# Constants of a decode kernel loaded at the end of the first key row instead of by a load of their own

## The chip, the cores and the metric

The kernel runs on one core of a Trainium2 chip. The metric is device time in microseconds (us) per execution; "span" is the time from the first to the last event in a profile, a little over 1 us less. Engines are called as in the profile: PE (matrix multiply, with PEld for its weight loads), DVE, ACT (ScalarE), POOL, and SP (SyncE), which here only issues loads. Loads are carried out by DMA engines, 16 by the page's count; a load has landed when an engine that waits for it sees its completion.

## The reference, cut to what matters

Two layers of attention and MLP decode one token. Each of 32 heads reads the last W = 4096 keys and values of 192 numbers each, so almost all the work is reading caches and weights.

```python
x = A_x                                   # 1 x 1 x 640, bf16
for layer in range(2):                    # the same weights and caches twice
    x = x + attention(layernorm(x), k_cache[:, :, -4096:], v_cache[:, :, -4096:], wq, wo)
    x = x + mlp(layernorm(x), w_gate, w_up, w_down)
```

## The kernel before

Heads are worked on in 16 pairs. SBUF holds one array, `big`, with seven slots of UNIT = 14208 bf16 per partition (28416 bytes) and a shared region behind them. A slot holds a pair's wq and keys ("a"), or its values and wo ("b"). Two thirds of the bytes come in loads ("c") that fill two neighbouring slots at once: keys of pair p and values of pair p-1, in rows of 56832 bytes on each of 128 partitions. SP issues every load in one fixed order, each as soon as its slots are free.

One small load is different. The constants (identity, masks, selectors and x itself, 241 bf16 or 482 bytes per partition) go into a tile of their own, on ScalarE's queue:

```python
cst = sb("cst", [P, CE + CE % 2], BF16)                   # CE = 241
big = sb("big", [P, NSLOT * UNIT + ME], BF16, 256)
M0 = NSLOT * UNIT                                          # start of the shared region
...
pg.dma(q_dma(cst[:, 0:CE], cx), "x", wr=[res("cst")], q="adma")   # ScalarE's queue
while seq_pos[0] < 2:                                      # SP: keys of pair 0, then ("c", 0, 1)
    assert try_load(seq[seq_pos[0]])
    seq_pos[0] += 1
pg.op("pool", ... tensor_copy(slot(2, wo of pair 0), slot(5, wo of pair 0)))
...
# first users of the constants: they start pair 0
pg.op("dve", ... wsel from pm, rd=[res("cst")])
pg.op("dve", ... xT[0] and its sum from x_in, rd=[res("cst")], ...)
```

Pair 0 then goes: layernorm sums, projection of q (Q), scores (QK), maximum, exp, transposed exp (ET). Pair 1 repeats this, with the values of pair 0 in between (PV). Slots for the fourth load come free only when pair 1's softmax has passed and pair 0's output has been projected.

## Time and profile before

| | before |
|---|---|
| time, median of the first 3 executions | 513.91 us (513.4 to 514.08) |
| span | 512.3 us |
| busy: PE, DVE, ACT | 51%, 20%, 17% |
| read from memory | 218.2 MB at a mean of 426 GB/s |
| first use of the constants | 15.31 us |
| first key load landed, after its issue at 0.0 | 11.0 us |

These lines of the page show what bounds the kernel. The slices are 40 equal parts of the span; a 9 is 90% busy or more. The queue lines give packets, MB and the share of the DMA engines' time; q1 is SP's queue and q10 is ScalarE's.

```profile
span 512.3 us, 8586 instructions
...
DMA  9999999999999999999999999999999999999996
...
GB/s 422 435 423 426 423 426 436 426 426 448 444 430 435 432 430 430 430 426 453 409 413 418 409 441 431 434 435 426 435 448 444 439 426 426 431 436 417 427 429 283
...
q1 hardware_dynamic: 9506, 218.14, 99.2%
...
q10 hardware_dynamic: 144, 0.06, 0.0%
```

In slices of this size the DMA engines are busy 90% or more until the last one. Busy time by stretch says it for the long middle part (columns: stretch, length, busy us and instructions of PE, PEld, DVE, ACT, POOL, granted PE clock, DMA share, GB/s):

```profile
0.00:30.00 30.00, 7.30 (x80) 4.01 (x84) 4.50 (x22) 3.45 (x6) 2.04 (x6) 1.00 1.01 426
...
60.00:250.00 190.00, 88.28 (x1179) 43.86 (x1183) 31.29 (x111) 27.70 (x55) 1.07 (x12) 0.59 1.00 433
```

The timeline of the start (start us, length us, engine, line, operation, count, and in brackets the idle time before and what ended it). The last line is SP's issue of the fourth load.

```profile
0.78 0.38 ACTq L217 DMA_DIRECT2D cst<-in_cx_dram  x1
...
15.31 0.17 DVE L364 TENSOR_SCALAR sc<-cst 128x2 f32<-128x2 bf16 x1 [13.20 <-DMA cst<-in_cx_dram]
...
17.43 2.75 PE L432 MATMUL scores<-big,qs 128*32 128x512 bf16 x24 [0.35 <-DVE qs L420]
...
24.72 0.38 PE L464 MATMUL bank<-cst,e_sb 128*128 128x8 bf16 x8 [1.98 <-ACT e_sb L458]
...
27.91 0.56 PE L414 MATMUL bank<-sh,big 128*128 128x1 bf16 x15 [2.81 <-DMA big<-in_uc_dram]
...
33.82 1.47 PE L494 MATMUL o<-big,et_sb 128*2 128x384 bf16 x32
...
37.98 0.33 SPq L217 DMA_DIRECT2D big<-in_uc_dram  x1
```

The constants, issued at 0.78 us, release DVE at 15.31 us, though the keys of pair 0 were there at about 11. Pair 0's scores start at 17.43 and its ET ends at about 25.1. PE then waits 2.81 us for the second load, and pair 1 starts at 27.91.

The chain of waits (start, length, what), its first load and the next:

```profile
1.17 44.86 DMA big<-in_uc_dram
...
57.90 21.63 DMA big<-in_uc_dram
```

It starts with 45 us of loads. Pair 0 is not on it.

### The profile page before, as it was taken

How to read it: one execution, taken by the hardware profiler on the slowest of the kernel's cores; microseconds unless marked ns; L12 is line 12 of the kernel's file. 1: busy time of each engine (PE TensorE's matmuls, PEld its weight loads, DVE VectorE, ACT ScalarE, POOL GpSimd, SP SyncE). 2: the span in 40 equal slices, each digit the busy share in tenths (PEclk: the TensorE clock that was granted, in tenths of full speed). 3: DMA queues.
4: the chain of work that ended last, by engine and by line, in shares of the span. 5: the costliest groups of instructions: out<-in, count | busy, mean ns of one | idle time of the engine just before them, and what ended most of it. 6: DMA issues, size and time to landing. Idle time of an engine off the chain costs nothing.

```text
span 512.3 us, 8586 instructions
## 1 busy us (share of the span) xinstructions
PE 260.4 (51%) x3716; PEld 137.8 (27%) x3716; DVE 102.3 (20%) x386; ACT 85.2 (17%) x173; POOL 4.3 (1%) x31
## 2 busy tenths in 40 slices
PE   0452456333534464436576767775726343534655
PEld 0220222121212231223234434432312121212334
DVE  0221322112210221112121333231202112210312
ACT  1110111011101111011121023221201011101221
POOL 0010000000000000000000000000000000000000
PEclk9995655567755565666555568865665557755575
DMA  9999999999999999999999999999999999999996
GB/s 422 435 423 426 423 426 436 426 426 448 444 430 435 432 430 430 430 426 453 409 413 418 409 441 431 434 435 426 435 448 444 439 426 426 431 436 417 427 429 283
DMA packets 9670, 218.47 MB, mean 426 GB/s; under 512 B 1201, under 2 KB 1586, under 8 KB 4658
## 3 DMA queue, kind: packets, MB, share of 16 engines
q1 hardware_dynamic: 9506, 218.14, 99.2%
q8 instruction: 13, 0.21, 0.1%
q10 hardware_dynamic: 144, 0.06, 0.0%
q14 instruction: 7, 0.06, 0.0%
HBM read 218.20 MB, written 0.00 MB: 426 GB/s over the span
## 4 chain that ended last, share of the span: by engine, by line
DMA 63%; PE 24%; DVE 7%; ACT 3%; issue 2%; SPq 1%; DVEq 0%; POOL 0%; ACTq 0%; POOLq 0%
DMA big<-in_uc_dram 54%; PE scores L432 8%; PE o L494 7%; DMA big<-in_wd_dram 6%; DMA big<-in_wu_dram 4%; DVE sc L442 3%; PE bank L448 2%; PE bank L414 2%; ACT e_sb L458 2%; PE bank L529 1%; PE bank L464 1%; ACT diag L445 1%; SPq L217 1%; DVE sc L477 1%; DVE qs L420 1%
## 5 line engine op out<-in xcount | busy, mean ns | idle before, releaser
L432 PE MATMUL scores<-big,qs 128*32 128x512 bf16 x744 | 82.7, 613 | 10.3 <-DVE qs L420 9.5
L414 PE MATMUL bank<-sh,big 128*128 128x1 bf16 x465 | 17.2, 166 | 133.1 <-DMA big<-in_uc_dram 130.7
L494 PE MATMUL o<-big,et_sb 128*2 128x384 bf16 x1024 | 73.7, 453 | 7.2 <-DMA big<-in_uc_dram 4.1
L445 ACT ACTIVATE diag<-cst,sc 128x128 f32<-128x128 bf16 x32 | 12.8, 401 | 308.3 <-DVE sc L442 295.1
L442 DVE TENSOR_REDUCE sc<-scores 128x1 f32<-128x1024 f32 x31 | 37.9, 1224 | 78.3 <-PE scores L432 78.3
L414 PEld LDWEIGHTS bank<-sh,big 128*128 128x128 bf16 x465 | 14.8, 104 | 136.2 <-DMA big<-in_uc_dram 113.6
L448 PE MATMUL bank<-diag,sc 128*128 128x128 f32 x64 | 22.1, 441 | 46.6 <-ACT diag L445 46.6
L458 ACT ACTIVATE e_sb<-scores,sc 128x1024 bf16<-128x1024 f32 x31 | 37.4, 1206 | 41.6 <-DVE sc L453 39.3
L420 DVE TENSOR_TENSOR qs<-bank,cst 128x96 bf16<-128x96 f32 x30 | 7.7, 258 | 162.0 <-PE bank L414 162.0
L494 PEld LDWEIGHTS o<-big,et_sb 128*2 128x2 bf16 x1024 | 27.3, 104 | 41.2 <-issue 25.8
L432 PEld LDWEIGHTS scores<-big,qs 128*32 128x32 bf16 x744 | 24.1, 132 | 43.7 <-issue 31.2
L448 PEld LDWEIGHTS bank<-diag,sc 128*128 128x128 f32 x64 | 13.8, 269 | 72.7 <-ACT diag L445 70.5
L501 ACT CAST o_sb<-o 128x384 bf16<-128x384 f32 x64 | 29.4, 475 | 19.8 <-PE o L494 19.6
L529 PE MATMUL bank<-sh,big 128*128 128x1 bf16 x480 | 17.2, 165 | 15.4 <-DVE sh L518 15.4
L468 DVE CAST et_sb<-bank 128x64 bf16<-128x64 f32 x32 | 7.2, 225 | 68.1 <-PE bank L464 68.1
L529 PEld LDWEIGHTS bank<-sh,big 128*128 128x128 bf16 x480 | 14.6, 99 | 17.9 <-DVE sh L518 12.5
L449 DVE TENSOR_REDUCE sc<-bank 128x2 f32<-128x128 f32 x32 | 9.3, 292 | 42.8 <-PE bank L448 42.8
L464 PE MATMUL bank<-cst,e_sb 128*128 128x8 bf16 x256 | 11.7, 169 | 8.2 <-ACT e_sb L458 8.1
L464 PEld LDWEIGHTS bank<-cst,e_sb 128*128 128x128 bf16 x256 | 8.9, 101 | 24.0 <-issue 17.1
L475 PE MATMUL o<-sc 128*128 128x2 f32 x62 | 14.2, 298 | 0.6 <-ACT o_sb L501 0.6
L475 PEld LDWEIGHTS o<-sc 128*128 128x128 f32 x62 | 12.1, 244 | 2.2 <-ACT o_sb L501 1.3
L477 DVE RECIPROCAL sc<-o 64x1 f32<-64x1 f32 x62 | 10.2, 165 | 10.5 <-PE o L475 8.7
(81 smaller groups left out, 110.9 us busy)
## 6 DMA issues: line engine op xcount, KB each, us to landing
big<-in_uc_dram SPq DMA_DIRECT2D x20, 7104.0 KB, 22.7
big<-in_uc_dram SPq DMA_DIRECT2D x11, 3552.0 KB, 20.1
big<-in_uc_dram SPq DMA_DIRECT2D x2, 3072.0 KB, 17.9
big<-in_uc_dram SPq DMA_DIRECT2D x8, 480.0 KB, 6.3
big<-in_uc_dram SPq DMA_DIRECT2D x1, 2784.0 KB, 12.2
big<-in_uc_dram SPq DMA_DIRECT2D x1, 2304.0 KB, 10.3
big<-in_uc_dram SPq DMA_DIRECT2D x1, 2048.0 KB, 10.8
big<-in_wg_dram SPq DMA_DIRECT2D x2, 960.0 KB, 15.9
```

Of the source, the lines that this page charges most:

```text
L414: ins = t.matmul(qe[:, i:i + 1], lhsT=w[:, c * 2 * DH + c0:c * 2 * DH + c0 + P], rhs=xq[:, c:c + 1], start=(c == 0), stop=(c == DC - 1))
L432: ins = t.matmul(sc_x[1 + b][32 * j:32 * j + 32, :], lhsT=qs[:, y, k, :], rhs=slot(sa, WQE + k * W + (4 * b + j) * 512, 512), start=(k == ...
L442: pg.op("dve", lambda v: v.reduce_max(out=mx, in_=sc_x[0][:], axis=AX.X), wr=[res("mx")], ex=sc_x[3:5])
L445: pg.op("act", lambda a: a.mul(out=diag[:], in_=ident, mul=mx), rd=[res("cst"), res("mx")], wr=[res("diag")])
L448: pg.op("pe", lambda t: t.matmul(dmx[:, 0:P], lhsT=ones_f, rhs=diag[:], start=True, stop=True), rd=[res("diag"), res("ones")], ex=[rb[2]])
L458: pg.op("act", lambda a: a.activation(out=e_sb[:], in_=sc_x[0][:], func=ACT.Exp, bias=nbias, scale=srs_c, accum_out=rowsum), rd=[res("nbia ...
L464: ins = t.matmul(qe[:, 0:2 * NB].rearrange("p (r x) -> p r x", r=2)[:, :, 4 * b:4 * b + 4], lhsT=e_sb[:, b * P:(b + 1) * P], rhs=sel, star ...
L475: pg.op("pe", lambda t: t.matmul(sm, lhsT=ones_f, rhs=rs2[z], start=True, stop=True), rd=[res(f"rs2{z}"), res("ones")], wr=[res("rsum")], ...
L477: rb[bk].last["dve"] = pg.op("dve", lambda v, h=h: v.reciprocal(out=Rn[z][64 * h:64 * h + 64], in_=sm[64 * h:64 * h + 64, h:h + 1]), rd=[r ...
L494: ins = t.matmul(o8[h][32 * j:32 * j + 2, 0:2 * DH].rearrange("p (a d) -> p a d", a=2), lhsT=et_sb[:, z, h * NB + 2 * u:h * NB + 2 * u + 2 ...
L501: pg.op("act", lambda a, h=h: a.copy(out=o8_sb[:, :, h * DH:(h + 1) * DH], in_=o8[h][:, 0:2 * DH].rearrange("p (a d) -> p a d", a=2)), wr= ...
L529: ins = t.matmul(yT[:, j:j + 1], lhsT=wo[:, c * D + j * P:c * D + (j + 1) * P], rhs=oTb[z][:, c:c + 1], start=False, stop=(c == 2), skip_g ...
```

## The change

The intent: let the constants come with the first key load, so that the small load on the second queue goes away and pair 0 can start earlier. The array gets a gap of 256 bf16 behind the slot of the first keys, the host writes the constants behind the first key row in memory, and the first key load becomes 241 columns longer.

```diff
-    cst = sb("cst", [P, CE + CE % 2], BF16)
-    big = sb("big", [P, NSLOT * UNIT + ME], BF16, 256)
-    M0 = NSLOT * UNIT
+    GAP = -(-CE // P) * P
+    big = sb("big", [P, NSLOT * UNIT + GAP + ME], BF16, 256)
+    M0 = NSLOT * UNIT + GAP
+    cst = big[:, 5 * UNIT:5 * UNIT + GAP]
...
     def slot(s, o, n):
-        return big[:, PLACE[s] * UNIT + o:PLACE[s] * UNIT + o + n]
+        o += PLACE[s] * UNIT + (GAP if PLACE[s] > 4 else 0)
+        return big[:, o:o + n]
...
+            ext = CE if it[1:] == (0, 0) else 0
-            pg.dma(q_dma(slot(s, o0, UNIT - o0), a_in(it[2], o0)), ... wr=[rslot[s]])
+            pg.dma(q_dma(slot(s, o0, UNIT + ext - o0), a_in(it[2], o0, UNIT + ext)), ...
+                   wr=[rslot[s]] + ([res("cst")] if ext else []))
...
-    pg.dma(q_dma(cst[:, 0:CE], cx), "x", wr=[res("cst")], q="adma")
...
-    return dict(cx=cx, uc=uc, ...)
+    uc[0][:, UNIT:UNIT + CE] = cx
+    return dict(uc=uc, ...)
```

More of the change, by code (lines that the diff above doesn't have):

```diff
@@ L109, in decode_kernel @@
 @with_exitstack
-def decode_kernel(ctx: ExitStack, nc, cx: bass.AP, uc: bass.AP,
+def decode_kernel(ctx: ExitStack, nc, uc: bass.AP,
                   wg_d: bass.AP, wu_d: bass.AP, wd_d: bass.AP, out: bass.AP):
@@ L263, in try_load @@
             first = min(ss, key=PLACE.get)
-            assert abs(PLACE[ss[0]] - PLACE[ss[1]]) == 1 and first == ss[p % 2]
+            assert abs(PLACE[ss[0]] - PLACE[ss[1]]) == 1 and first == ss[p % 2] and PLACE[first] != 4
             pg.dma(q_dma(slot(first, 0, 2 * UNIT), uc[p]), f"c{l}{p % 2}", wr=[rslot[x] for x in ss])
@@ L271, in try_load @@
             o0 = WQE if it[1:] == (1, 3) else 0
-            pg.dma(q_dma(slot(s, o0, UNIT - o0), a_in(it[2], o0)), f"c{it[1]}{it[2] % 2}" if it[1:] in ((0, 15), (1, 4), (1, 5), (1, 6), (1, 13)) else f"a{it[1]}_{it[2]}", wr=[rslot[s]])
+            ext = CE if it[1:] == (0, 0) else 0
+            assert not ext or PLACE[s] == 4
+            pg.dma(q_dma(slot(s, o0, UNIT + ext - o0), a_in(it[2], o0, UNIT + ext)), f"c{it[1]}{it[2] % 2}" if it[1:] in ((0, 15), (1, 4), (1, 5), (1, 6), (1, 13)) else f"a{it[1]}_{it[2]}", wr=[rslot[s]] + ([res("cst")] if ext else []))
         elif k == "b":
@@ L869, in decode_kernel @@
     emit("dma", nc.sync, 1, NFIRST, known_sp)
-    emit("adma", nc.scalar)
     with nc.Block() as block:
@@ L939, in _layout @@
     cx[:, C_X:] = x.reshape(DC, P).T
-    return dict(cx=cx, uc=uc, wg=blk(wg), wu=blk(wu), wd=wdn)
+    uc[0][:, UNIT:UNIT + CE] = cx
+    return dict(uc=uc, wg=blk(wg), wu=blk(wu), wd=wdn)
 def kernel(**inputs):
```

## The prediction

> **What bounds the kernel.** The load stream. The page shows a span of 512.3 us, 218.2 MB read at a mean of 426 GB/s, and DMA at 9 tenths or more in every slice but the last; PE is busy 51%, DVE 20%, ACT 17%. Of the chain of waits DMA has 63%; most other pieces end in a slot release that lets the next load be issued. Those loads are issued early enough: in 60 to 480 us (busy time by stretch) the DMA share is about 1.00, and the load issued at 57.9 us takes 21.6 us, though 7104 KB at 433 GB/s need 16.8 us: it queued. Compute has slack; only bytes, packets, gaps in the stream, or the last microseconds after it can move the time.
>
> **Removed.** One load on ScalarE's queue: 60.2 KB in 128 rows of 482 bytes, with 16 completion writes (144 packets, 0.7% of the first 30 us: 0.21 us). It lands 14.5 us after its issue at 0.78 us: DVE's first use of cst (L364) waits 13.2 us and starts at 15.31. The first key load, issued at 0.0, lands after 11.0 us, so the constants, not the keys, start pair 0. [...]
>
> **Added.** 482 bytes on each of 128 rows of the first key load (28416 to 28898 bytes). At 27 bytes/ns per DMA engine (estimate: 433 GB/s over 16) that is 18 ns a row, 0.14 us per engine. Slots 5, 6 and the shared region move by 512 bytes; no compute instruction changes shape, and later loads are the same.
>
> **On the critical path.** The constants should come with the keys at about 11.1 us, so L364 and the first projection start some 4.2 us earlier (first scores at 13.2, not 17.43). But pair 0 ends at 25.5 us today and PE then waits 2.8 us, until 27.9, for the second load (timeline). That landing does not depend on pair 0, and everything after it does: pair 1's projection, the copy on POOL, the slot release at 38 us. So the 4.2 us become a longer wait before 27.9. What stays is the DMA engines' net work: 0.21 less, 0.14 more, about 0.1 us of 514, below the spread (513.4 to 514.08).
>
> **Prediction.** 513.8 us, 8 times in 10 between 513.0 and 514.5. Faster by over 2%: 0.01; within 2%: 0.98; slower by over 2%: 0.01.
>
> **What would show it.** Right: L364's instruction starts near 11 us; PE's wait before the second projection is about 7 us and ends within 0.4 us of 27.9; the fourth load is still issued near 38 us; the chain again starts with DMA until about 46 us. Wrong: L364 still near 15 us, or the second load lands over 0.5 us away from 27.9 and that shift is kept to the end.
>
> **What would make it wrong.** (1) Small rows cost more than their own 27 ns, by switching queues: DMA moved 361 GB/s in 2 to 5 us, 455 in 10 to 30. If the second queue causes that start, up to 1 us could be won. (2) Rows of 28898 bytes, or shifted slots, could write slower. (3) Fixed costs of a second DMA queue at start or end. [...]

Two passages are cut where marked: a sentence that explained the constants' lateness by a rule, and a fourth way to be wrong, on an earlier fall of PE's clock. Neither is a term of the forecast's sum, which stands whole: 0.21 us less and 0.14 us more DMA work, net about 0.1 us of 514, forecast 513.8.

## The result, and the profile after

| | before | changed |
|---|---|---|
| median, 6 executions each | 513.42 us (513.03 to 514.08) | 513.23 us (513.06 to 514.61) |
| ratio, 95% interval | | 0.9998 (0.9985 to 1.0011) |
| again later, beside three variants | 513.65 us (9 executions) | 513.61 us (5), ratio 1.0002 (0.9989 to 1.0016) |

A ratio is the mean time of one kernel's fast executions over that of the other's of the same rounds, so it is not quite the ratio of the medians. The two kernels are equal within 0.2%. A gain or loss of up to about 0.7 us would not be seen in these times; the account below rests on the traces and on the experiments.

The same lines of the page of the changed kernel (q10 is gone from it, q1 has 0.06 MB more in the same number of packets):

```profile
span 512.1 us, 8585 instructions
...
GB/s 427 431 423 426 423 435 427 426 463 440 431 426 431 427 435 431 426 453 444 397 420 420 403 438 439 434 427 425 450 435 444 431 431 431 445 427 411 430 426 280
...
q1 hardware_dynamic: 9506, 218.20, 99.2%
```

Its busy time by stretch, first 30 us:

```profile
0.00:30.00 30.00, 7.33 (x80) 4.01 (x84) 4.50 (x22) 3.44 (x6) 2.03 (x6) 1.00 1.00 426
```

In the first 30 us the stream moves 426 GB/s, exactly as before. Lines of the timeline's start (source lines are 3 higher than before, so DVE L367 answers to L364):

```profile
11.12 0.17 DVE L367 TENSOR_SCALAR sc<-big 128x2 f32<-128x2 bf16 x1 [9.01 <-DMA big<-in_uc_dram]
...
13.23 2.75 PE L435 MATMUL scores<-big,qs 128*32 128x512 bf16 x24 [0.35 <-DVE qs L423]
...
20.53 0.38 PE L467 MATMUL bank<-big,e_sb 128*128 128x8 bf16 x8 [1.98 <-ACT e_sb L461]
...
27.89 0.56 PE L417 MATMUL bank<-sh,big 128*128 128x1 bf16 x15 [6.98 <-DMA big<-in_uc_dram]
...
34.10 2.73 PE L497 MATMUL o<-big,et_sb 128*2 128x384 bf16 x32
...
39.01 0.33 SPq L219 DMA_DIRECT2D big<-in_uc_dram  x1
```

The constants arrive 4.19 us earlier (11.12 against 15.31), pair 0's ET starts 4.19 us earlier (20.53 against 24.72), and PE's wait before pair 1 grows from 2.81 to 6.98 us: by 4.17 us. Pair 1 starts at 27.89 instead of 27.91. All of the gain is absorbed by one wait.

The chain of waits starts as before:

```profile
1.17 44.53 DMA big<-in_uc_dram
...
56.73 22.55 DMA big<-in_uc_dram
```

One thing went the other way. The fourth load was issued at 39.01 us, 1.03 us later than before, mainly because pair 1's PV took 2.73 us for the same 32 matmuls that took 1.47. More on this below.

### The profile page after: what moved, and what is told of

Its sections match the earlier page's. It is cut to its first block, busy times and chain, and to the rows that moved or that the text cites. A ratio compares the mean times of both kernels' runs of the same rounds, so it can differ in the third digit from the quotient of the medians.

```text
span 512.1 us, 8585 instructions
## 1 busy us (share of the span) xinstructions
PE 256.5 (50%) x3716; PEld 135.4 (26%) x3716; DVE 101.8 (20%) x386; ACT 85.5 (17%) x173; POOL 4.2 (1%) x31
## 3 DMA queue, kind: packets, MB, share of 16 engines
q1 hardware_dynamic: 9506, 218.20, 99.2%
## 4 chain that ended last, share of the span: by engine, by line
DMA 64%; PE 22%; DVE 8%; ACT 3%; issue 2%; SPq 1%; DVEq 0%; POOL 0%; ACTq 0%; POOLq 0%
DMA big<-in_uc_dram 54%; PE scores L435 8%; DMA big<-in_wd_dram 6%; PE o L497 6%; DMA big<-in_wu_dram 4%; DVE sc L445 3%; PE bank L451 2%; ACT e_sb L461 2%; PE bank L417 2%; PE bank L532 1%; PE bank L467 1%; ACT diag L448 1%; SPq L219 1%; DVE sc L480 1%; DVE qs L423 1%
## 5 line engine op out<-in xcount | busy, mean ns | idle before, releaser
L448 ACT ACTIVATE diag<-big,sc 128x128 f32<-128x128 bf16 x32 | 12.8, 401 | 312.5 <-DVE sc L445 304.5
L423 DVE TENSOR_TENSOR qs<-bank,big 128x96 bf16<-128x96 f32 x30 | 7.7, 258 | 167.8 <-PE bank L417 167.8
L532 PEld LDWEIGHTS bank<-sh,big 128*128 128x128 bf16 x480 | 14.5, 98 | 17.1 <-DVE sh L521 12.0
L467 PE MATMUL bank<-big,e_sb 128*128 128x8 bf16 x256 | 11.6, 169 | 8.6 <-ACT e_sb L461 8.4
L467 PEld LDWEIGHTS bank<-big,e_sb 128*128 128x128 bf16 x256 | 8.9, 100 | 23.9 <-issue 17.4
L480 DVE RECIPROCAL sc<-o 64x1 f32<-64x1 f32 x62 | 10.2, 164 | 9.2 <-PE o L478 7.6
## 6 DMA issues: line engine op xcount, KB each, us to landing
big<-in_uc_dram SPq DMA_DIRECT2D x1, 3612.2 KB, 11.1
```

The source lines that it names most:

```text
L448: pg.op("act", lambda a: a.mul(out=diag[:], in_=ident, mul=mx), rd=[res("cst"), res("mx")], wr=[res("diag")])
L467: ins = t.matmul(qe[:, 0:2 * NB].rearrange("p (r x) -> p r x", r=2)[:, :, 4 * b:4 * b + 4], lhsT=e_sb[:, b * P:(b + 1) * P], rhs=sel, star ...
L480: rb[bk].last["dve"] = pg.op("dve", lambda v, h=h: v.reciprocal(out=Rn[z][64 * h:64 * h + 64], in_=sm[64 * h:64 * h + 64, h:h + 1]), rd=[r ...
L532: ins = t.matmul(yT[:, j:j + 1], lhsT=wo[:, c * D + j * P:c * D + (j + 1) * P], rhs=oTb[z][:, c:c + 1], start=False, stop=(c == 2), skip_g ...
```

## The experiments

The theory has two parts. First, pair 0 has slack: its early start only lengthens the wait for the second load, and the stream of loads is the bound. Second, the constants were late because each of their rows waited for one row of the large load on the other queue. The rivals: the early start does win time, and the longer row or the moved slots lose it again; the 14.5 us are a latency of ScalarE's queue; the stream has idle time.

Eleven variants ran, one of them the changed kernel again. All results agreed with the reference.

### Delays put back in: 8, 20 and 40 memsets

To take back the early start alone, dependent memsets were put on DVE between the arrival of the constants and the layernorm sum. N is 8, 20 or 40, later 12, 14 and 16.

```diff
+    res("dly").w = rb[5].last["dve"]
+    for i in range(N):
+        pg.op("dve", lambda v: v.memset(o8[1][:], 0.0), rd=[res("dly")], wr=[res("dly")], ex=[rb[5]])
     pg.op("dve", ... xT[0] and its sum from x_in ...)
```

Expected of N = 8: 

> The changed kernel with 8 dependent memsets of 128x512 on DVE (about 0.51 us each in the trace of before, some more with a wait between) put between the arrival of the constants and the first layernorm step: it takes back the 4.2 us of early start and keeps the new load. Theory (the start has slack until the second load lands): first scores near 17.5 to 18 us, PE's wait for the second load shrinks from 7 to about 2.5 us and still ends at 27.9, time the same as the changed kernel within 0.3 us (513.2). Rival (the early start wins time, and something else in the change, the longer row or the moved slots, loses as much): the time rises by 3 to 4 us to about 517.

Expected of N = 20: 

> The same with 20 memsets, 10 to 12 us of delay. Theory: pair 0 now ends about 4 us after the second load has landed, so pair 1 and the issue of the fourth load come some 4 us later (about 43 instead of 39 us). The stream has loads queued until the third lands at about 45.7 us[...], so this is at the edge: 513.2 to 515. Rival that every delay beyond the 7 us of wait is paid in full: about 517.

Expected of N = 40: 

> The same with 40 memsets, 20 to 24 us of delay. Theory: the fourth load can only be issued at about 53 to 56 us, the stream runs dry at about 43 to 45 us, and that gap of 9 to 13 us is never won back: 522 to 527 us, with a DMA share clearly under 1 between 44 and 58 us. Rival (compute has slack everywhere and the stream catches up): under 516.

In the traces successive memsets start 0.667 us apart, so the delays are 5.3, 13.3 and 26.7 us, more than the 0.5 to 0.6 us apiece that the expectations assumed.

The timeline with 8 memsets, scores of pair 0 and start of pair 1:

```profile
18.52 2.75 PE L438 MATMUL scores<-big,qs 128*32 128x512 bf16 x24 [0.35 <-DVE qs L426]
...
27.88 0.56 PE L420 MATMUL bank<-sh,big 128*128 128x1 bf16 x15 [2.01 <-DMA big<-in_uc_dram]
```

With 8 the scores of pair 0 start at 18.52 us, the wait is 2.01 us, pair 1 starts at 27.88, and the time is 513.64 us against 513.66 before (ratio 1.0004, 0.9990 to 1.0018; as an absolute time it lies 0.14 us above the expected range). Undoing the early start costs nothing, so it had won nothing, and nothing else in the change was hiding a gain. (The profiled execution of this variant happened to be its slowest, 515.75 us, so only its first 60 us are used here.)

With 20 the time is 516.41 us (ratio 1.0054), with 40 it is 530.52 us (1.0331). Both are above their expected ranges, because the delays were longer than assumed. The rival's 517 for 20 memsets lies near, but only because it too was reckoned with the shorter delay: with the measured 13.3 us, all beyond the 7 us of wait paid in full would be 6.3 us, and 2.75 were paid. The DMA share between 40 and 60 us shows where the time went. Busy time by stretch of before, 20 and 40 memsets:

```profile
40.00:60.00 20.00, 8.26 (x104) 4.08 (x104) 5.14 (x16) 2.54 (x5) 0.09 (x1) 0.59 0.96 413
```

```profile
40.00:60.00 20.00, 12.45 (x169) 6.42 (x169) 6.32 (x24) 4.69 (x9) 0.09 (x1) 0.76 0.85 351
```

```profile
40.00:60.00 20.00, 12.58 (x169) 6.36 (x170) 5.80 (x22) 4.61 (x10) 0.09 (x1) 0.89 0.24 95
```

The DMA share falls from 0.96 to 0.85 and 0.24. With 40 memsets, 20 us x (0.96 - 0.24) = 14.4 us of the DMA engines' time is lost in that stretch, out of 16.9 us on the clock; some of the gap lies past 60 us. POOL's markers that the fourth load and the last such load have landed, first in the changed kernel and then with 40 memsets:

```profile
62.65 0.09 POOL L255 MEMSET sc<- 1x1 f32 x1 [16.75 <-DMA big<-in_uc_dram]
...
487.37 0.09 POOL L255 MEMSET sc<- 1x1 f32 x1 [16.75 <-DMA big<-in_uc_dram]
```

```profile
79.58 0.09 POOL L255 MEMSET sc<- 1x1 f32 x1 [34.00 <-DMA big<-in_uc_dram]
...
504.28 0.09 POOL L255 MEMSET sc<- 1x1 f32 x1 [16.72 <-DMA big<-in_uc_dram]
```

The fourth load lands 16.93 us later and the last one 16.91 us later. What the stream lost there it never won back.

### A useless load of 1776 KB

```diff
+    pg.dma(q_dma(slot(2, 0, UNIT // 2), uc[1][:, 0:UNIT // 2]), "spare", wr=[rslot[2]])   # behind the second load
```

> The changed kernel with one useless load of 1776 KB (1.82 MB) into an empty slot, queued behind the second load. At 433 GB/s it takes 4.2 us of the stream, as much as the early start won for pair 0. Theory (the stream is the bound from the first load to the last): plus 4.2 us, about 517.4. Rival (the stream has idle time that such a load would fill): plus less than 2 us.

Measured: 517.99 us against 513.66, 4.33 us more (ratio 1.0088, 1.0072 to 1.0103); the estimate was 4.2. So 4.2 us of bytes cost 4.3 us, while 4.2 us of earlier start are worth nothing. At this place the stream has no idle time to fill. (POOL's copy waited 4.14 us for the useless load, whose slot it writes, but the fourth load was still issued at 39.16 us, so that wait is not the cost.)

### Why the constants were late: the same bytes in twice as many rows

On the kernel before:

```diff
-    pg.dma(q_dma(cst[:, 0:CE], cx), "x", wr=[res("cst")], q="adma")
+    pg.dma(q_dma(cst[:, 0:120], cx[:, 0:120]), "x", q="adma")
+    pg.dma(q_dma(cst[:, 120:CE], cx[:, 120:CE]), "x", wr=[res("cst")], q="adma")
```

> The kernel before with its load of constants on ScalarE's queue cut into two loads of half the columns (120 and 121): the same bytes in 16 instead of 8 small rows per DMA engine. Theory (each DMA engine takes turns between the two queues row by row, so each small row waits for one large one): the second half lands about 8 turns later, each as long as a row of 56.8 KB, 2.1 us, so at about 32 us instead of 15.3. Pair 0 then starts 21 us later than it could, as in the 40-memset run, and the time rises by some 8 to 12 us. Rival (the 14.5 us are a latency of ScalarE's queue, or due to the bytes): the constants land at 15 to 17 us and the time stays at 513.4.

The queue line of this variant's page:

```profile
q10 hardware_dynamic: 288, 0.06, 0.1%
```

First use of the constants in its timeline:

```profile
32.36 0.17 DVE L365 TENSOR_SCALAR sc<-cst 128x2 f32<-128x2 bf16 x1 [30.22 <-DMA cst<-in_cx_dram]
```

Landing times of the two loads into cst, from the view of that tile:

```profile
DMA to landing us min/median/max: 14.7/22.9/31.1
```

The packets doubled from 144 to 288. In the trace of the kernel before the 144 are 128 of 482 bytes, the rows, and 16 of 4 bytes, which come last (14.44 to 14.94 us). The first half, with half the bytes, still took 14.7 us to land; the second took 31.1. First use moved from 15.31 to 32.36 us: 17.05 us for 8 more rows per DMA engine, 2.13 us a row. A 7104 KB load is 8 rows of 56832 bytes per engine, so at 433 GB/s one such row lasts 16.8 / 8 = 2.10 us; in the trace of the kernel before these rows take a median of 2.10 us too, and those of 28416 bytes 1.05 us. One small row waits for one large row; neither the bytes nor a fixed latency accounts for it. The trace of the kernel before agrees. Its queue lines from 8 to 16 us count as many packets on q10 as on q1, 96 and 96. Its records have the 128 small rows in groups of 16. The first packets of the first six groups start at 4.81, 5.88, 6.95, 8.02, 9.10 and 10.17 us, 1.07 us apart, beside rows of 28416 bytes; those of the seventh at 10.40, while 4-byte packets of q1 pass (10.2 to 10.7); beside rows of 56832 bytes the eighth follows at 12.32 and the 4-byte packets at 14.44, 1.92 and 2.12 us later. So a packet is one row here, but for 16 of 4 bytes in each load: q1's 9506 packets in the kernel before are 144 for each of its 66 loads, and two more. The time was 524.41 us (ratio 1.0211, 1.0196 to 1.0227), within the expected 8 to 12 us more: this late, constants do cost time: the fourth load was issued only at 52.81 us and landed at 73.54, 10.66 us later than before.

### The own load on SyncE's queue

On the kernel before, with the constants' load moved behind the first key load in SP's order:

```diff
-    pg.dma(q_dma(cst[:, 0:CE], cx), "x", wr=[res("cst")], q="adma")
     while seq_pos[0] < 2:
         assert try_load(seq[seq_pos[0]])
+        if seq_pos[0] == 0:
+            pg.dma(q_dma(cst[:, 0:CE], cx), "x", wr=[res("cst")])
```

> The kernel before with its own load of constants issued on SyncE's queue, directly behind the first key load; no moved slots and no longer row. Theory (only the second queue makes the constants late): they land at 11.2 to 11.6 us, DVE starts there, the time is the same as both kernels (513.2, within 0.4). Rival (a load of its own of small rows is late wherever it is issued): 14 us or later.

First use of the constants in the timeline of this variant:

```profile
11.13 0.17 DVE L365 TENSOR_SCALAR sc<-cst 128x2 f32<-128x2 bf16 x1 [8.99 <-DMA cst<-in_cx_dram]
```

The constants are there at 11.13 us, as in the changed kernel (11.12), with no gap and no longer row. Time 513.62 us, ratio 1.0000 (0.9987 to 1.0014). So this small load was late (15.31 us) only on another queue than the large rows.

### The layout alone, and the changed kernel again

The gap, the moved slots and the moved shared region, with the constants still loaded on ScalarE's queue:

> The kernel before with only the layout of the change: the constants in a gap of 512 bytes behind slot 4, slots 5 and 6 and the shared region moved by 512 bytes; the load of constants is still its own on ScalarE's queue. Theory: first use of the constants at 15.3 us as before and the same time (513.4 within 0.3). Rival (the moved slots cost or save something): a difference clear of noise, over 0.1%.

Measured: first use at 15.30 us, 513.78 us, ratio 1.0006 (0.9992 to 1.0019). No difference clear of noise.

> The changed kernel again, beside the kernel before and the three variants on one chip. Theory: within 0.1% of the kernel before, 513.2 to 513.5. Rival (the change wins up to 1 us, lost in the noise of the first comparison): 512.4 and a ratio under 0.9985.

Measured: 513.61 us, ratio 1.0002 (0.9989 to 1.0016); first use at 11.05 us, pair 1 at 27.79. In ratio both held, as did that of the load on SyncE's queue. As absolute times the three medians lie 0.02 to 0.11 us above their ranges; the kernel before stood at 513.65 in these rounds.

### How much slack: 14, then 12 and 16 memsets

> The changed kernel with 14 memsets, which at the 0.667 us apiece measured in the runs with 8, 20 and 40 are 9.3 us of delay. From those runs: a 7104 KB load issued into an idle stream landed 20.7 to 21.0 us after its issue (45.53 to 66.5, 58.87 to 79.6 us), and the fourth load lands at 62.6 to 62.9 us when it is not held up, so it may be issued as late as about 41.8 us. With 14 memsets pair 1 should start 2.6 to 2.7 us after the second landing (at 30.5 instead of 27.9) and the fourth load be issued at about 41.5 us. Theory: no time lost, the fourth load still lands at 62.6 to 63, 513.4 to 513.9. Rival (delay beyond the wait for the second load is paid in full, or in the proportion of the run with 20, 2.75 of 6.7 us): 514.7 to 516.3.

It did not go as written. Pair 1 started at 32.07 us, not 30.5, and the fourth load was issued at 43.05 and landed at 63.84. The time was 513.72 us (ratio 1.0010, 0.9996 to 1.0023): unclear. In the trace 1.37 of the nearly 1.6 us of surplus sit in a single DVE instruction (1.53 us instead of 0.16), which led to two more runs.

> 12 memsets, 8.0 us of delay. In the run with 14 one DVE instruction, the bias step of pair 0, took 1.53 instead of 0.16 us: it began at 28.30 us, inside POOL's copy (28.03 to 29.81), and ended at 29.83. That put the issue at 43.05 instead of 41.5 us, past the edge of 41.8. With 12 the step falls at about 27.0 us, before the copy. Theory (the edge is at an issue of about 41.8 us): pair 1's projection at about 29.2 us, the fourth load issued at 40 to 40.5 us and landed at 62.6 to 62.9; 513.3 to 513.7. Rival (delays past the wait are paid from the start): fourth landing at 63.3 or later.

> 16 memsets, 10.7 us of delay. Theory of the collision (DVE's bias step waits for POOL's copy to end at about 29.8 us): the step begins at about 29.6 us and is hardly stretched, so pair 1 starts at 31.8 to 32.1 us, as late as with 14 memsets though the delay is 1.33 us longer; the issue is at 42.8 to 43.1 us, the fourth load lands at 63.6 to 64.0, the time is that of the run with 14 within 0.4 us. Rival (the 1.53 us of the run with 14 were a chance event of one run): pair 1 at 31.9 all the same, but the 14-memset run should then be faster than this one by about 1 us in its other executions.

The timelines of the runs with 12, 14 and 16 memsets, in this order: POOL's copy (in the second), the DVE instruction in question (L459, the bias step), SP's issue of the fourth load, and POOL's marker that it has landed:

```profile
26.87 0.16 DVE L459 CUSTOM_DVE_ANT_0 sc<-sc 128x2 f32<-128x2 f32 x1
...
40.38 0.33 SPq L219 DMA_DIRECT2D big<-in_uc_dram  x1
...
62.89 0.09 POOL L255 MEMSET sc<- 1x1 f32 x1 [16.79 <-DMA big<-in_uc_dram]
```

```profile
28.03 1.78 POOL L359 COPY big<-big 128x1920 bf16<-128x1920 bf16 x1
...
28.30 1.53 DVE L459 CUSTOM_DVE_ANT_0 sc<-sc 128x2 f32<-128x2 f32 x1
...
43.05 0.33 SPq L219 DMA_DIRECT2D big<-in_uc_dram  x1
...
63.84 0.09 POOL L255 MEMSET sc<- 1x1 f32 x1 [17.96 <-DMA big<-in_uc_dram]
```

```profile
29.55 0.18 DVE L459 CUSTOM_DVE_ANT_0 sc<-sc 128x2 f32<-128x2 f32 x1
...
43.05 0.33 SPq L219 DMA_DIRECT2D big<-in_uc_dram  x1
...
63.98 0.09 POOL L255 MEMSET sc<- 1x1 f32 x1 [17.97 <-DMA big<-in_uc_dram]
```

With 12 memsets (8.0 us of delay) the issue is at 40.38 us, the landing at 62.89 as in the kernel before (62.88), and the time is 513.54 us, equal to before in the same rounds (ratio 1.0002). With 16 the issue is at 43.05, the landing 1.10 us later than before, and the time 514.49 us (ratio 1.0026, 1.0012 to 1.0040). Five runs with an idle stream (14, 16, 20 and 40 memsets, two halves) give the time from issue to landing of such a load: 43.05 to 63.84 and to 63.98, 45.53 to 66.51, 58.87 to 79.58, 52.81 to 73.54, so 20.7 to 21.0 us. The latest issue that loses nothing is therefore about 62.9 - 20.9 = 42.0 us (worked out). The kernel before issues at 37.98, 4.0 us ahead of that; the changed kernel at 39.01, 3.0 us ahead.

The DVE step behaved as the theory of a collision says: 0.16 us when it ended before POOL's copy began (12), 1.53 us when it began inside the copy, ending at 29.83 where the copy ends at 29.81 (14), and 0.18 us when it began near the copy's end, ending at 29.73 where the copy ends at 29.72 (16). With 12 another DVE step began inside the copy (L475, at 29.04): it took 0.69 us, against 0.22 with 14 and 16, and ended at 29.73, where the copy ends at 29.71. Not every DVE instruction was held: the cast just before it (L474), which began inside the copy at 28.90, took 0.23 us, as with 14 and 16. What sets the two kinds apart, no run shows. In the runs with 14 and 16 the issue then falls at the same 43.05 us. The expectation that their times agree within 0.4 us failed: the ratios are 1.0010 and 1.0026, 0.8 us apart, nearer to the 1 us that the rival of a chance event forecast. The two runs stood in different rounds and their intervals overlap, so this decides nothing. The collision is shown in the profiled execution with 14; whether it happens in each execution is open. The step starts 0.3 us after the copy there, and the landing that starts the copy moved by more than that between runs (27.79 to 28.59 us).

### What these runs do not settle

Pair 1's PV took 1.47 to 1.76 us in three kernels (before, layout alone, 8 memsets; PE had waited 2.0 to 2.8 us before pair 1) and 2.73 us in four (the changed kernel twice, SyncE's queue, useless load; waits of about 7 us). By itself this would point to the length of PE's wait. But PV also took 2.73 us with 12, 14, 16 and 20 memsets, where PE's last waits before pair 1 were 2.0 (3.35 with 14) and 0.41 us, and only 1.76 and 1.78 us after the same waits of 2.0 and 0.41 us with two halves and 40 memsets. Nor does the granted clock of the profile tell the forms apart: from 34 to 38 us it is 1.00 both before, with the fast PV, and after, with the slow one, and with 20 memsets it was 1.00 from 38 to 44 us, where that slow PV lay (40.76 us). So no run tells what decides. In the changed kernel it moved the issue by 1.0 us, inside the slack, and so did not reach the time.

## Why the prediction was right

A forecast of no change can be met by several mechanisms, so each of its steps is compared with what was seen.

- **The bound.** Right. Extra bytes cost their full time (4.33 us for an estimate of 4.2), and a gap in the stream is kept to the end (16.93 us at the fourth load, 16.91 at the last). PE's clock did not show: six executions of the changed kernel had mean granted clocks of 0.612 to 0.669, and the ones at the two ends took 513.09 and 513.36 us.
- **The constants arrive with the keys.** Right: 11.12 us (predicted about 11.1), first scores at 13.23 (13.2).
- **The gain turns into a wait.** Right: 6.98 us before pair 1 (about 7), ending at 27.89 (within 0.4 of 27.9). The 8-memset run shows it by intervention.
- **The constants' load, not the keys, was late**. Right: 2.13 us for each row added on ScalarE's queue, and first use at 11.13 us instead of 15.31 with the same load on SP's.
- **Net DMA work of 0.1 us.** Too small to be seen. The layout alone, the own load on SyncE's queue and the whole change all measure 1.000 within 0.2%.
- **"The fourth load is still issued near 38 us."** Off by 1.0 us: 39.01. The prediction took pair 1's compute as unchanged, and its PV ran slower after the longer wait. The slack, still 3.0 us, hid it.
- **The ways to be wrong.** The slow start of the stream was not due to the second queue (2 to 5 us moved 395 GB/s without it instead of 361, but the first 30 us 426 GB/s with and without it); longer row and moved slots cost nothing measurable; and no fixed cost of a second queue showed. As to PE's clock, the granted clock in 30 to 60 us was 0.94 and 0.97 in the two profiles of the changed kernel, against 0.70 before; with the load on SyncE's queue, the same early start, it was 0.50 from 20 to 30 us and 0.66 from 30 to 40, and the time was the same (median 513.62 us).

## What to carry to other kernels

Before making a step earlier, find the event that releases the step after it: here pair 1 waited for a load, and 4.2 us won ahead of it only lengthened that wait. In a kernel whose loads never pause, ask of a change what it does to bytes and to the latest harmless issue of the next load; here an issue had 3 to 4 us in hand, a delay of pair 0 in the changed kernel became costly somewhere between 8.0 and 10.7 us, and the gap then stayed to the end. A small load that is needed early is better put on the same queue as the large ones, in its place in their order: on a second queue each of its rows waited here for about one large row (1.07 us beside rows of 28416 bytes, 2.13 us beside 56832).
